# K chunks in pairs of neighbouring places, w4 in runs of seven rows

## The chip, the cores and the metric

The kernel runs on one core of one Trainium2 chip. The metric is the time of one execution in microseconds, as the device measures it; the time of a kernel is the median of its runs.

## The reference

Four blocks run one after the other over a batch of 8, with one query position: attention with a cached K and V, an MLP, and both once more with the same weights and the same caches. All inputs are bf16.

```python
def _A_ref(x, k_cache, v_cache, wq, wo):       # D 448, Hq 16, Hkv 8, Sk 4096, Dh 256
    q = (x @ wq)...                             # 16 heads, two for each of 8 K/V heads
    scores = jnp.einsum("bhqd,bhkd->bhqk", q, k) * (Dh ** -0.5)
    p = _softmax(scores, axis=-1)
    o = jnp.einsum("bhqk,bhkd->bhqd", p, v)
    return o... @ wo
def _B_ref(x, w1, w2, w3, w4):
    ...                                         # hs: shifts along S, zero for S = 1
    x1 = x + hs
    h2 = _gelu(_layernorm(x1, axis=-1) @ w3) @ w4      # w3 448 x 1792, w4 1792 x 448
    return x1 + h2
x = A_x
x = x + _A_ref(_layernorm(x, axis=-1), ...)
x = x + _B_ref(_layernorm(x, axis=-1), ...)
x = x + _A_ref(_layernorm(x, axis=-1), ...)
x = x + _B_ref(_layernorm(x, axis=-1), ...)
```

K and V of one batch row are 16.8 MB each, so the two passes over the caches could ask for 537 MB. Since S is 1, the shifted quarters of the MLP's first half are all zero, and w1 and w2 take no part.

## The kernel before

**Units and chunks.** The heads are taken in pairs of K/V heads: four pairs (gp 0 to 3) for each of 8 batch rows b, in two passes (ps 0 and 1). A unit (ps, b, gp) has four K chunks and four V chunks of 1 MB: 128 partitions of 8192 B. Chunk c of K holds rows 16c to 16c+15 of the 64 consecutive rows that each partition has of K; two neighbouring chunks c and c+1 are therefore one run of 16384 B per partition in HBM. In SBUF lie 17 places of a chunk's size side by side in one tile, `places_t`; two chunks can be loaded by one DMA if their places are neighbours.

**What is kept.** For the head pairs 2 and 3 (`keep`) the K chunks and most V chunks of pass 0 stay in their places, or in part in PSUM, and pass 1 of the same batch row uses them from there; these items need no load (`here`). Head pairs 0 and 1 are loaded in both passes.

**The order.** `items` is a list of 522 items, written out at build time by `block`, `first_kept` and `weights`: for each unit its K chunks and, some way behind, its V chunks, with those of other units between; an item with kv 2 is a block of wq or wo. For each batch row, after the units of pass 0, a stretch of V chunks alone follows (`narrow`), during which the dependent chain of that row (`chain`: softmax denominators, wo, layernorm, w3, gelu, w4, q of pass 1) is worked off in small steps between halves of V chunks. Most of those V chunks are loaded in two halves (`halved`).

**The planner.** All loads are issued by the sync engine (SP), in the order of `loads`, which is `items` without those that are kept. `emit_loads` (line 930) runs after each item and issues loads as long as places are free. `both_for` (line 900) decides on a pair: the two chunks must be within the next three loads, two neighbouring places must be free or come free within `AHEAD = 4` items, and at least `QUEUED = 7` loaded chunks must be waiting for their use; then the places are held, and nothing else is issued until both are free. If not, `place_for` (line 873) takes a single place, and tries to hold a neighbour of it for the mate, so that the score products can still read both chunks as one operand. An item gives its place back when its last product has been issued (lines 1463 to 1476); a pair of chunks whose scores are formed together (`late`) gives both back after the second.

**What an item does.** A loaded K chunk is turned in place by VectorE (L1009, three instructions). Scores are formed by TensorE (L1024): 32 matmuls with 256 columns for two chunks in neighbouring places, 64 with 128 columns for two others; `paired` says which units form them two by two. ScalarE takes the exponentials (L1033). A V chunk is multiplied in 16 matmuls (L1092), those of the last units in 32 (L1108), where V is the weight operand and every second column of it is taken.

**The MLP.** w3 lies in SBUF as three blocks of 128 rows with all 1792 columns, and a last block in which the 64 remaining rows stand twice, one half of the columns on the upper and one on the lower 64 partitions (`split_tile`). `wblk` gives the 128 columns 128c to 128c+127 of block fc as the weight operand; there are 14 x 4 = 56 such products in `mlp_hidden` (L471 and following; through `wide`, L180, for one batch row) and in the last MLP (L1550). w4 lies as `w4_sb[p, c, :]` = row 128c + p, loaded at line 1159:

```python
nc.sync.dma_start(w4_sb[:], B_w4.rearrange("(c p) d -> p c d", p=128))
```

The hidden values of column group c stand on the 128 partitions and meet `w4_sb[:, c]`, so the order of the columns in w3's products and that of the rows in w4 must agree.

Of the kernel before, what the change touches and what calls it, by code (L numbers as in the profile page):

```python
# [17 lines left out]
def kernel(  # L18
# [27 lines left out]
    nc = tc.nc  # L46
# [3 lines left out]
    Dh = A_k_cache.shape[3]  # L50
# [10 lines left out]
    NC = 17  # L61
# [160 lines left out]

    def rows_to_cols(row, nb):

# [236 lines left out]
    def mlp_hidden(b0, nb):  # L464

        yield from norm(xT[:, :, b0 : b0 + nb], nb, True)
        h_ps = room_ps("h", nb)
        for c in range(HC):
            for fc in range(4):
                w, xi = wblk(w3_sb, F, c, fc)  # L470
                if nb == 1:  # L471
                    wide(h_ps[:, c : c + 1], w, xbs(1)[:, xi, :], fc == 0, fc == 3)
                    continue
                nc.tensor.matmul(
                    h_ps[:, c * nb : c * nb + nb],
                    w,
                    xbs(nb)[:, xi, :],
                    start=(fc == 0),
                    stop=(fc == 3),
                )  # L480
            if c in (4, 9, HC - 1) if nb == 1 else c % 7 == 6:
                yield 0 if c == HC - 1 else None
        g_t = chn.tile([128, HC * MID], FP32, tag="g")
        hh = g_t[:, 0 : HC * nb]
        g0 = g_t[:, HC : 2 * HC] if nb == 1 else misc[:, 456 : 456 + HC * nb]
        if nb == 1:
            HT_t = chn.tile([128, HC, 1], BF16, tag="HT")
            HT = HT_t[:]
        else:
            HT = HTw[:, :, b0 : b0 + nb]  # L490

        nc.vector.tensor_scalar_mul(hh, h_ps, 0.5)
        nc.vector.scalar_tensor_tensor(g0, hh, 4 * 0.044715, hh, ALU.mult, ALU.mult)
        nc.vector.scalar_tensor_tensor(g0, g0, 1.0, hh, ALU.add, ALU.mult)
        nc.scalar.activation(g0, g0, ACT.Tanh, scale=2 * 0.7978845608028654)
        yield 0
        nc.vector.scalar_tensor_tensor(
            HT,
            g0.rearrange("p (c b) -> p c b", b=nb),
            1.0,  # L500
            hh.rearrange("p (c b) -> p c b", b=nb),
            ALU.add,
            ALU.mult,
        )
        yield 2
        return HT
# [337 lines left out]
    where = {}  # L844

    held = {}
    AHEAD = 4
    QUEUED = 7

    def paired(n, c):  # L850

        ps, _, gp = tasks[n]
        return gp in keep or tasks[n] in saved or tasks[n] in final_units[:2] + begin[1:]

    def late(it):

# [13 lines left out]
    free_at = [-1] * NC  # L870
    now = [0]

    def place_for(it):

        n, kv, c = it
        if it in held:
            p = held.pop(it)
            if p not in places:
                held[it] = p
                return None  # L880
            places.remove(p)
        else:
            open_ = [p for p in places if p not in held.values()]
            if not open_:
                return None
            p = open_[0]
            if kv == 0 and c % 2 == 0 and paired(n, c):
                two = [
                    (max(free_at[q], now[0]), k, p1, q)
                    for k, p1 in enumerate(open_)  # L890
                    for q in (p1 + 1, p1 - 1)
                    if 0 <= q < NC and q not in held.values() and free_at[q] <= now[0] + AHEAD
                ]
                if two:
                    _, _, p, q = min(two)
                    held[n, 0, c + 1] = q
            places.remove(p)
        return p

    def both_for(it):  # L900

        n, kv, c = it
        mate = (n, 0, c + 1)
        if it not in held:
            if kv or c % 2 or not paired(n, c) or mate not in loads[:3]:
                return None
            open_ = [p for p in range(NC) if p in places or free_at[p] >= 0]
            two = [
                (max(free_at[q] if q not in places else -1 for q in (p, p + 1)), p)
                for p in open_  # L910
                if p + 1 in open_ and not {p, p + 1} & set(held.values())
            ]
            two = [t for t in two if t[0] <= now[0] + AHEAD]
            if not two or sum(used_at[i] > now[0] for i in where if i in used_at) < QUEUED:
                return None
            p = min(two)[1]
            held[it], held[mate] = p, p + 1
        if held.get(mate) != held[it] + 1:
            return None
        return held[it], mate  # L920

    def taken(it, p):

        where[it] = p
        n, kv, c = it
        if stays(it):
            where[tasks[n][1:], it[1:]] = p
        free_at[p] = again[tasks[n][1:], kv, c] if tasks[n][0] == 0 and stays(it) else used_at[it]

    def emit_loads(most=None):  # L930
        n = 0
        while loads and places and n != most:
            it = loads[0]
            both = both_for(it)
            if both:
                p, mate = both
                if p not in places or p + 1 not in places:
                    break
                for i, q in ((it, p), (mate, p + 1)):
                    loads.remove(i)  # L940
                    places.remove(q)
                    del held[i]
                    taken(i, q)
                _, b, gp = tasks[it[0]]
                nc.sync.dma_start(
                    places_t[:, p * PB : (p + 2) * PB],
                    A_k_cache[b, 2 * gp : 2 * gp + 2]
                    .rearrange("g s d -> (g s) d")
                    .rearrange("(p u z) d -> u p (z d)", u=2, z=32)[it[2] // 2],
                )  # L950
                n += 1
                continue
            p = place_for(it)
            if p is None:
                break
            del loads[0]
            taken(it, p)
            t, kv, c = it
            _, b, gp = tasks[t]
            dst = slots[p]  # L960
            n += 1
            if kv == 2:
                load_weights(dst, gp, b)
                continue
            rows = (A_v_cache if kv else A_k_cache)[b, 2 * gp : 2 * gp + 2].rearrange(
                "g s d -> (g s) d"
            )
            if kv:
                src = rows.rearrange("(a p y) d -> a p (y d)", a=4, y=16)[c]
            else:  # L970
                src = rows.rearrange("(p x y) d -> x p (y d)", x=4, y=16)[c]
            if halfway(it):
                nc.sync.dma_start(dst[:, 0 : PR * Dh], src[:, 0 : PR * Dh])
                nc.sync.dma_start(rest_t[:], src[:, PR * Dh :])
            elif loads and it not in halved:
                nc.sync.dma_start(dst, src)
            else:
                for y in range(2):
                    nc.sync.dma_start(
                        dst[:, 8 * Dh * y : 8 * Dh * (y + 1)], src[:, 8 * Dh * y : 8 * Dh * (y + 1)]  # L980
                    )

    def load_tail(dst, src):

# [171 lines left out]
        A_wo[WI * 128 :].rearrange("(h p j) d -> p h (j d)", p=128, j=2),  # L1156
    )
    load_split(w3_sb, B_w3, F)
    nc.sync.dma_start(w4_sb[:], B_w4.rearrange("(c p) d -> p c d", p=128))
    run(norm(xT[:], Bn, False))  # L1160

    gens, pairs_done, p_of = [], {}, {}
# [109 lines left out]
    for idx, it in enumerate(items):  # L1272
# [190 lines left out]
        if kv == 2:  # L1463
            if gp == "q" or rows is not None:
                places.append(p)
        elif not (ps == 0 and stays(it)):
            if (ps, gp, kv, c) == (1, keep[1], 1, homes[0]):
                where[(b, part[0]), part[1:]] = p
                moves.extend(part_words(slot))
            elif (ps, gp, kv, c) == (1, keep[1], 1, homes[1]):  # L1470
                where[(b, inner[0]), inner[1:]] = p
                moves.extend(inner_words(slot))
            elif not late(it):
                places.append(p)
            elif c % 2:
                places.extend([where[n, 0, c - 1], p])
# [69 lines left out]
    for f0, f1 in ((0, 3), (3, 4)):  # L1546
        for c in range(HC):
            for fc in range(f0, f1):
                w, xi = wblk(w3_sb, F, c, fc)
                nc.tensor.matmul(  # L1550
                    h_ps[:, c * nb : c * nb + nb],
                    w,
                    xe[:, xi, :],
                    start=(c + fc == 0),
                    stop=(fc == 3),
                    skip_group_check=True,
                )
# [80 lines left out]
```

## Time and profile before

| | |
|---|---|
| median of three runs | 1040.58 us (1037.08 to 1041.28) |
| the profiled execution | 1038.57 us, its span 1036.0 us |
| read from HBM | 419.63 MB, 405 GB/s over the span |
| DMA packets | 73472 |
| busy: PE, DVE, ACT, POOL | 668.8, 597.9, 211.5, 16.3 us |
| mean granted clock of TensorE | 0.614 |

The span goes from the first to the last instruction of the core; the execution's time also holds what lies around it. In the groups of instructions, PE is a matmul and PEld the load of its weight operand, "busy" is the time of a group together and the mean is that of one instruction, overlaps counted. SPq is the queue of the sync engine: an issue of a DMA stands there at the time at which SP got to it, waits included. The views by stretch give, for each 10 us, the busy time of every engine, then the granted clock, the mean share of the 16 DMA engines that had a packet, and GB/s. The records of single packets (start, duration, size, queue) lie behind that share.

### The profile page before, as it was taken

How to read it: one execution, taken by the hardware profiler on the slowest of the kernel's cores; microseconds unless marked ns; L12 is line 12 of the kernel's file. 1: busy time of each engine (PE TensorE's matmuls, PEld its weight loads, DVE VectorE, ACT ScalarE, POOL GpSimd, SP SyncE). 2: the span in 40 equal slices, each digit the busy share in tenths (PEclk: the TensorE clock that was granted, in tenths of full speed). 3: DMA queues.
4: the chain of work that ended last, by engine and by line, in shares of the span. 5: the costliest groups of instructions: out<-in, count | busy, mean ns of one | idle time of the engine just before them, and what ended most of it. 6: DMA issues, size and time to landing. Idle time of an engine off the chain costs nothing. (4 is left out here: it accounts for less than half of the span.)

```text
span 1036.0 us, 29893 instructions
## 1 busy us (share of the span) xinstructions
PE 668.8 (65%) x13219; PEld 429.1 (41%) x13219; DVE 597.9 (58%) x1407; ACT 211.5 (20%) x685; POOL 16.3 (2%) x27
## 2 busy tenths in 40 slices
PE   3154545875677557766775677567756774677775
PEld 2022322553345334533453345335533552345555
DVE  7054577258725971597259725782597259725582
ACT  1011111141214120412041214121412141214110
POOL 0000000000000000000000000000000000000000
PEclk9975555565667566655665565566555665556555
DMA  9999999999999999999999999999999999999994
GB/s 361 396 425 422 423 422 419 393 421 419 419 401 421 422 417 382 419 422 419 401 415 425 417 402 411 421 417 388 418 420 418 401 419 423 417 402 408 413 419 198
DMA packets 73472, 421.56 MB, mean 407 GB/s; under 512 B 7544, under 2 KB 13440, under 8 KB 43904
## 3 DMA queue, kind: packets, MB, share of 16 engines
q1 hardware_dynamic: 73296, 419.66, 99.1%
q8 instruction: 103, 1.69, 0.7%
q14 instruction: 25, 0.20, 0.0%
q10 hardware_dynamic: 48, 0.01, 0.0%
HBM read 419.63 MB, written 0.01 MB: 405 GB/s over the span
## 5 line engine op out<-in xcount | busy, mean ns | idle before, releaser
L1009 DVE STREAM_TRANSPOSE places<-places 128x512 uint32<-128x512 uint32 (+1 forms) x576 | 455.5, 854 | 58.8 <-DMA places<-in_A_k_cache_dram 58.6
L1024 PE MATMUL sc<-places,qbd 128*8 128x256 bf16 (+1 forms) x5248 | 248.8, 342 | 175.4 <-DVE places L1009 168.5
L1092 PE MATMUL o<-places,ptw 128*8 128x256 bf16 x3808 | 243.7, 380 | 111.5 <-DMA places<-in_A_v_cache_dram 82.2
L1024 PEld LDWEIGHTS <-qbd 128*8 128x8 bf16 x5248 | 134.0, 105 | 247.0 <-DVE places L1009 130.6
L1092 PEld LDWEIGHTS <-ptw 128*8 128x8 bf16 x3968 | 103.9, 102 | 175.1 <-issue 99.0
L1033 ACT ACTIVATE p_n<-sc 128x256 bf16<-128x256 f32 x128 | 95.5, 746 | 341.2 <-PE sc L1024 335.7
L1267 ACT COPY ptw<-psv 128x32 bf16<-128x32 bf16 x248 | 53.1, 227 | 175.0 <-PE o L1092 173.0
L415 DVE CAST qbd<-misc 32x16 bf16<-32x16 f32 (+1 forms) x184 | 30.8, 167 | 63.2 <-PE misc L409 61.4
L592 PE MATMUL misc<-R_t,o_t 128*128 128x4 f32 (+1 forms) x212 | 45.5, 321 | 29.2 <-DVE qbd L415 12.8
L592 PEld LDWEIGHTS misc<-R_t,o_t 128*128 128x128 f32 x212 | 41.2, 271 | 45.2 <-issue 17.3
L1082 ACT CAST psv<-misc 128x128 bf16<-128x128 f32 x64 | 17.0, 265 | 198.8 <-PE misc L1075 198.8
L532 DVE RECIPROCAL rz<-misc 128x4 f32<-128x4 f32 (+1 forms) x55 | 9.7, 176 | 80.4 <-PE misc L529 43.6
L1060 ACT COPY places<-store 128x1024 bf16<-128x1024 bf16 x40 | 40.2, 1029 | 11.2 <-PE o L1092 10.7
L529 PE MATMUL misc<-zm,one 128*128 128x4 f32 (+1 forms) x110 | 28.0, 326 | 15.0 <-DVE zm L521 12.6
L529 PEld LDWEIGHTS misc<-zm,one 128*128 128x128 f32 x110 | 23.2, 263 | 30.8 <-DVE zm L521 15.9
L180 PEld LDWEIGHTS <-w_sb 128*128 128x128 bf16 x896 | 27.5, 104 | 15.7 <-issue 15.7
L1033 ACT ACTIVATION_READ_ACCUMULATOR p_n<-sc 128x1 f32 x128 | 33.8, 264 | 0.0
L546 ACT COPY o_t<-o 128x256 f32<-128x256 f32 x53 | 19.7, 373 | 49.5 <-PE o L1092 49.5
L295 POOL TENSOR_TENSOR t<-t,nhalf 128x2 f32<-128x2 f32 (+2 forms) x18 | 12.0, 669 | 955.5 <-DVE t L316 955.5
L1075 PEld LDWEIGHTS <-p_n 128*128 128x128 bf16 x256 | 11.9, 105 | 32.4 <-issue 20.9
L1055 DVE TENSOR_SCALAR store<-places 128x512 uint32<-128x512 uint32 x40 | 25.0, 679 | 0.0
L1075 PE MATMUL misc<-identb,p_n 128*128 128x32 bf16 x256 | 18.1, 191 | 10.3 <-ACT p_n L1033 6.8
(158 smaller groups left out, 358.7 us busy)
## 6 DMA issues: line engine op xcount, KB each, us to landing
places<-in_A_k_cache_dram SPq DMA_DIRECT2D x49, 2048.0 KB, 17.2
places<-in_A_v_cache_dram SPq DMA_DIRECT2D x194, 512.0 KB, 7.2
places<-in_A_k_cache_dram SPq DMA_DIRECT2D x94, 1024.0 KB, 12.0
places<-in_A_v_cache_dram SPq DMA_DIRECT2D x87, 1024.0 KB, 20.9
places<-in_A_wq_dram SPq DMA_DIRECT2D x7, 768.0 KB, 9.8
rest<-in_A_v_cache_dram SPq DMA_DIRECT2D x8, 640.0 KB, 18.5
places<-in_A_v_cache_dram SPq DMA_DIRECT2D x8, 384.0 KB, 14.8
wo_sb<-in_A_wo_dram SPq DMA_DIRECT2D x1, 2688.0 KB
```

Of the source, the lines that this page charges most:

```text
L180: nc.tensor.matmul(bass.AP(out.tensor, out.offset, [out.ap[0], (1, WIDE)]), w, x.to_broadcast([128, WIDE]), start=start, stop=stop, skip_g ...
L415: nc.vector.tensor_copy(qbd[32 * a : 32 * a + 32, :, g0 : g0 + ng, a, :], qs.rearrange("p e (f g u h) -> p (e f) u g h", f=2, u=2, h=2)[:, ...
L529: nc.tensor.matmul(z_ps, ones, zm[:], start=True, stop=True)
L592: nc.tensor.matmul(ot_ps[:, j], o_sb[:].rearrange("p (i j) -> p j i", j=2)[:, j], R, start=True, stop=True)
L1009: nc.vector.transpose(w, w)
L1024: nc.tensor.matmul(sc[32 * k : 32 * k + 8, 128 * (x % 2) : 128 * (x % 2 + nx)], qbd[:, ep, gp % 2].rearrange("p a h -> p (a h)"), v, start ...
L1033: nc.scalar.activation(p_sb[:, :, :, 2 * u : 2 * u + 2].rearrange("p t i x -> p x t i"), sc[:, 0:256].rearrange("p (x t i) -> p x t i", x= ...
L1055: nc.vector.tensor_single_scalar(kept_words.bitcast(U32), words.bitcast(U32), 0, op=ALU.bitwise_or)
L1060: nc.scalar.copy(words, kept_words.bitcast(BF16))
L1075: nc.tensor.matmul(pt_ps[:, t], p_sb[:, t].rearrange("p i x -> p (i x)"), cols, start=True, stop=True,)
L1092: nc.tensor.matmul(o_ps[32 * q : 32 * q + 8, :], ptz[:, at : at + 8], v[:, y * Dh : (y + 1) * Dh] if v2 is None or y < PR else v2[:, (y - ...
L1267: nc.scalar.copy(ptw[:, ring_of[it], :, 6:8], psv[slot_of[it[0]]][:, it[2]])
```

## The change

It has four parts.

- The planner. `place_for` and `both_for` go. `reserve` holds two neighbouring places for a pair if both are free or come free within `SOON = 8` items, and either both are free now or at least `QUEUED = 5` loaded chunks are waiting for use; the mate may stand up to three loads behind. While a pair is held and one of its places is not free, nothing is issued. A single load takes the free place with the fewest free neighbours (`pick`). Chunks 1 and 2 of a unit go together when chunk 1 was left single, the next load is chunk 2 and the next place is free.
- `paired` now holds for all units of `begin` and `final_units`.
- Kept K chunks in pass 1, whose scores are formed two by two after the first, give both places back at that time.
- w4 is loaded so that each partition has seven consecutive rows for each half of the 1792 rows, and `w3blk` takes every seventh column of w3: group c = 7u + j has columns 896u + j, 896u + j + 7, and so on.

```diff
+    def w3blk(c, fc):
+        u, j = divmod(c, HC // 2)
+        at = F // 2 * u if fc < 3 else 0
+        return w3_sb[:, fc * F + at + j : fc * F + at + F // 2 : HC // 2], (fc if fc < 3 else 4 - u)
...
-                w, xi = wblk(w3_sb, F, c, fc)
+                w, xi = w3blk(c, fc)
...
-    AHEAD = 4
-    QUEUED = 7
+    SOON = 8
+    QUEUED = 5
...
-        return gp in keep or tasks[n] in saved or tasks[n] in final_units[:2] + begin[1:]
+        return gp in keep or tasks[n] in saved or tasks[n] in final_units + begin
...
-    def place_for(it):
...
-    def both_for(it):
...
+    def open_places():
+        return [p for p in places if p not in held.values()]
+    def pick(open_):
+        return min(open_, key=lambda p: ((p - 1 in open_) + (p + 1 in open_), p))
+    def reserve(it, mate):
+        open_ = open_places()
+        taken_ = set(held.values())
+        def at(p):
+            return max(-1 if q in places else free_at[q] for q in (p, p + 1))
+        two = [
+            p
+            for p in range(NC - 1)
+            if not {p, p + 1} & taken_
+            and all(q in places or 0 <= free_at[q] <= now[0] + SOON for q in (p, p + 1))
+        ]
+        if not two:
+            return
+        p = min(two, key=lambda p: (at(p), sum(q in open_ for q in (p - 1, p + 2)) % 2, p))
+        queued = sum(used_at[i] > now[0] for i in where if i in used_at)
+        if at(p) <= now[0] or queued >= QUEUED:
+            held[it], held[mate] = p, p + 1
...
+    def load_k(it, p, n):
+        _, b, gp = tasks[it[0]]
+        rows = A_k_cache[b, 2 * gp : 2 * gp + 2].rearrange("g s d -> (g s) d")
+        nc.sync.dma_start(
+            places_t[:, p * PB : (p + n) * PB],
+            rows.rearrange("(p z) d -> p (z d)", z=64)[:, it[2] * PB : (it[2] + n) * PB],
+        )
...
     def emit_loads(most=None):
         n = 0
         while loads and places and n != most:
             it = loads[0]
-            both = both_for(it)
...
+            k, kv, c = it
+            mate = (k, 0, c + 1)
+            if kv == 0 and c % 2 == 0 and paired(k, c) and mate in loads[:4]:
+                if it not in held:
+                    reserve(it, mate)
+                if it in held:
+                    p = held[it]
+                    if p in places and p + 1 in places:
+                        del held[it], held[mate]
+                        taken(it, p)
+                        taken(mate, p + 1)
+                        load_k(it, p, 2)
+                        n += 1
+                        continue
+                    break
+            open_ = open_places()
+            if not open_:
+                break
+            p = pick(open_)
+            taken(it, p)
+            n += 1
+            if kv == 2:
+                load_weights(slots[p], tasks[k][2], tasks[k][1])
+            elif kv:
+                load_v(it, slots[p])
+            else:
+                both = c == 1 and (k, 0, 2) in loads[:2] and p + 1 in open_
+                if both:
+                    taken((k, 0, 2), p + 1)
+                load_k(it, p, 1 + both)
...
-    nc.sync.dma_start(w4_sb[:], B_w4.rearrange("(c p) d -> p c d", p=128))
+    nc.sync.dma_start(
+        w4_sb[:].rearrange("p (u j) d -> p u (j d)", u=2),
+        B_w4.rearrange("(u p j) d -> p u (j d)", u=2, p=128),
+    )
...
+            elif kv == 0 and kept_now:
+                if c % 2 == 0:
+                    places.extend([p, where[(b, gp), (0, c + 1)]])
             elif not late(it):
                 places.append(p)
...
-                w, xi = wblk(w3_sb, F, c, fc)
+                w, xi = w3blk(c, fc)
                 nc.tensor.matmul(
                     h_ps[:, c * nb : c * nb + nb],
```

V chunks are loaded as before, by the same DMAs (`load_v`).

More of the change, by code (lines that the diff above doesn't have):

```diff
@@ L871 @@
     now = [0]
-    def place_for(it):
[L875 to L898, printed above, removed]
@@ L900, in both_for @@
-    def both_for(it):
[L902 to L916, printed above, removed]
+    def open_places():
+        return [p for p in places if p not in held.values()]
@@ L917, in both_for @@
             held[it], held[mate] = p, p + 1
-        if held.get(mate) != held[it] + 1:
-            return None
-        return held[it], mate
     def taken(it, p):
@@ L928, in taken, with load_v @@
         free_at[p] = again[tasks[n][1:], kv, c] if tasks[n][0] == 0 and stays(it) else used_at[it]
+        if kv == 2 and tasks[n][1] is None:
+            free_at[p] = -1
+        loads.remove(it)
+        places.remove(p)
+    def load_k(it, p, n):
[5 more added lines that the diff above has]
+        )
+    def load_v(it, dst):
+        _, b, gp = tasks[it[0]]
+        rows = A_v_cache[b, 2 * gp : 2 * gp + 2].rearrange("g s d -> (g s) d")
+        src = rows.rearrange("(a p y) d -> a p (y d)", a=4, y=16)[it[2]]
+        if halfway(it):
+            nc.sync.dma_start(dst[:, 0 : PR * Dh], src[:, 0 : PR * Dh])
+            nc.sync.dma_start(rest_t[:], src[:, PR * Dh :])
+        elif loads and it not in halved:
+            nc.sync.dma_start(dst, src)
+        else:
+            for y in range(2):
+                nc.sync.dma_start(
+                    dst[:, 8 * Dh * y : 8 * Dh * (y + 1)], src[:, 8 * Dh * y : 8 * Dh * (y + 1)]
+                )
     def emit_loads(most=None):
@@ L933, in emit_loads @@
             it = loads[0]
-            both = both_for(it)
-            if both:
-                p, mate = both
-                if p not in places or p + 1 not in places:
-                    break
[L939 to L952, printed above, removed]
@@ L953, in emit_loads @@
-            p = place_for(it)
-            if p is None:
+            k, kv, c = it
[12 more added lines that the diff above has]
+                        continue
+                    break
@@ L955, in emit_loads @@
+            open_ = open_places()
+            if not open_:
                 break
-            del loads[0]
+            p = pick(open_)
             taken(it, p)
-            t, kv, c = it
-            _, b, gp = tasks[t]
-            dst = slots[p]
             n += 1
             if kv == 2:
[L963 to L967, printed above, removed]
@@ L968, in emit_loads @@
-            if kv:
-                src = rows.rearrange("(a p y) d -> a p (y d)", a=4, y=16)[c]
-            else:
[L971 to L981, printed above, removed]
+                load_weights(slots[p], tasks[k][2], tasks[k][1])
+            elif kv:
+                load_v(it, slots[p])
+            else:
+                both = c == 1 and (k, 0, 2) in loads[:2] and p + 1 in open_
+                if both:
+                    taken((k, 0, 2), p + 1)
+                load_k(it, p, 1 + both)
@@ L1158 @@
     load_split(w3_sb, B_w3, F)
-    nc.sync.dma_start(w4_sb[:], B_w4.rearrange("(c p) d -> p c d", p=128))
+    nc.sync.dma_start(
+        w4_sb[:].rearrange("p (u j) d -> p u (j d)", u=2),
+        B_w4.rearrange("(u p j) d -> p u (j d)", u=2, p=128),
+    )
     run(norm(xT[:], Bn, False))
```

## The prediction

> **What bounds the kernel now.** I read the slices of the page first, then the DMA queues and issues, the chain that ended last, the busy time by stretches of 10 us, the waits of the sync engine's queue, and the weight loads by shape.
>
> ```profile
> DMA  9999999999999999999999999999999999999994
> GB/s 361 396 425 422 423 422 419 393 421 419 419 401 421 422 417 382 419 422 419 401 415 425 417 402 411 421 417 388 418 420 418 401 419 423 417 402 408 413 419 198
> q1 hardware_dynamic: 73296, 419.66, 99.1%
> ```
>
> The 16 DMA engines have packets from the first slice to the last but one. The packet records add up: the durations of all packets, over 16 engines, make 1034.7 us of a span of 1036.0 us. No engine's busy time comes near that (PE 668.8, DVE 597.9). So the time is the sum of the packets, plus what stands after the last transfer:
>
> ```profile
> 1007.79 17.29 DMA places<-in_A_v_cache_dram
> ...
> 1028.49 1.64 PE store L1550 x56
> ...
> 1033.06 0.27 DVE places L1603
> ```
>
> The last data lands at 1025.1 us, and some 11 us of dependent work follow; in it stand the 56 products with w3 (L1550), 29 ns each. There, and only there, work of TensorE lies on the path for sure. Everything else matters through the DMA queue: how cheap its packets are, and whether it ever runs empty.
>
> ```profile
> places<-in_A_k_cache_dram SPq DMA_DIRECT2D x49, 2048.0 KB, 17.2
> ...
> places<-in_A_k_cache_dram SPq DMA_DIRECT2D x94, 1024.0 KB, 12.0
> ...
> w_sb<-in_B_w_dram SPq DMA_DIRECT2D x1, 1568.0 KB, 15.1
> ```
>
> A K chunk is 1 MB, 8192 B per partition and packet; a pair is one DMA of 128 packets of 16384 B. Of 192 K chunks that are loaded, 98 go in pairs now. The w4 load moves rows of 896 B, 1792 packets.
>
> **Part 1, more pairs.** I walked the lists of both planners over the 522 items (they depend on no time). The old rules give 49 pairs and 94 single chunks, as the rows above show; the new ones give 86 DMAs of two chunks (7 of them chunks 1 and 2 of a unit) and 20 singles: 37 DMAs become one where they were two. From the packet records, a mean packet of 8192 B on this queue takes 315.0 ns (23,168 of them) and one of 16384 B 616.9 ns (6,272). Each engine carries 8 packets of a chunk: two chunks cost 16 x 315.0 = 5040 ns, a pair 8 x 616.9 = 4935 ns. Saved: 105 ns a pair, and 9 ns for one semaphore packet per engine less: 114 ns x 37 = **4.2 us**. The medians (312 and 613) give 88 + 9 = 97 ns, 3.6 us. That the gap belongs to the packets and not to quiet stretches is seen within one stretch: from 60 to 160 us, where the queue is deep, the means are 314.2 and 616.6. I take the means over the run, since the singles that go lie in stretches of all kinds.
>
> **Part 2, w4 in runs of seven rows.** 1792 packets of 896 B at 46.1 ns over 16 engines make 5.2 us. They become 256 packets of 6272 B; the records show 5120 B at 200.5 ns and 8192 B at 315, so by a straight line 243 ns: 3.9 us. Saved: **1.3 us**, at 30 to 43 us of the span, where the DMA share stands at 1.04 to 1.07 and nothing else sets the pace.
>
> **Part 3, w3 read in every seventh column.** The number of weight loads and products stays (56 per use, ten uses). Whether a load that steps 14 bytes takes longer the trace does not show; it shows steps of 4 and 8 bytes:
>
> ```profile
> L592 PEld LDWEIGHTS misc<-R_t,o_t 128*128 128x128 f32 x212 | 41.2, 271 | 45.2 <-issue 17.3 <-ACT o_t L546 15.2 <-DVE R_t L575 6.8
> L180 PEld LDWEIGHTS <-w_sb 128*128 128x128 bf16 x896 | 27.5, 104 | 15.7 <-issue 15.7
> L529 PEld LDWEIGHTS misc<-zm,one 128*128 128x128 f32 x110 | 23.2, 263 | 30.8 <-DVE zm L521 15.9 <-issue 8.5 <-DVE qT L379 1.7
> L1108 PEld LDWEIGHTS <-places 128*128 128x128 bf16 x256 | 7.7, 105 | 5.0 <-DMA places<-in_A_v_cache_dram 4.8 <-issue 0.2
> ```
>
> L1108 reads every second bf16 column and takes 105 ns against 104 for packed w_sb; L592 reads every second f32 and takes 271 against 263 (L529). So 0 by the nearest rows, and that is what I take. It can't gain, since no load goes away. The upper end is a load that moves no faster than an f32 one: 41.2/212 = 194 ns of busy time each against 1.8/56 = 32 for w3 at the end; 162 ns x 56 = 9.1 us in the tail. In the eight rounds of the chain the 56 products stand between halves of V chunks, hidden as long as PE keeps up: from 293 to 303 us it is busy 8.4 of 10 us.
>
> The Trainium skill speaks against a price of nothing: by "SBUF — State Buffer", section "Door 1: The DMA port swizzle", memory lines are 16 bytes long and full bandwidth needs at least two hits in a line. A step of 14 bytes gives about one hit a line; steps of 4 and 8 bytes give four and two, and there the rows agree with it. (The page also counts 8 bf16 as a free step, so it can be read both ways.)
>
> **Part 4, the order and the holding back.** A pair now waits for two neighbouring places when five chunks are ahead and both places come free within 8 items, and while it waits, everything behind it on SP waits too, V chunks among them. What hides this is the queue's stock. For each DMA of the new order I took the end of the item that lets it go, as the trace has it, and counted what had been issued before it less what had landed. The thinnest place is at 646 us:
>
> ```profile
> 634.79 0.33 SPq L945 DMA_DIRECT2D places<-in_A_k_cache_dram  x1
> 635.17 1.86 SPq L976 DMA_DIRECT2D places<-in_A_k_cache_dram  x2
> 642.96 0.33 SPq L976 DMA_DIRECT2D places<-in_A_v_cache_dram  x1
> 647.53 0.33 SPq L945 DMA_DIRECT2D places<-in_A_k_cache_dram  x1
> ```
>
> Before the V issue at 642.96 the queue held 3.69 MB. The two chunks of L976 at 635.17 become a pair that waits until 645.8, and the V stands behind it: 3.69 - 2.10 - 2.84 us x 0.42 MB/us = 0.4 MB, 1.0 us of work left when it goes out. The next thinnest such places have 0.95, 1.13, 1.34, 1.51, 1.67 and 1.80 MB (2.3 to 4.3 us). None is empty, so no stall. A thin stock by itself costs little: the stretch at 550 us, where 1.8 MB stood, ran at 416 GB/s against 420. For 12 such places of some 5 us each, 1% is 0.6 us; I take 0.5.
>
> Against it, kept K chunks give their two places back after the first of them and not one by one. Where the narrow V stretch ends, the old order ran thin, and the new one issues earlier there:
>
> ```profile
> 620.00:630.00 10.00, 7.68 (x158) 5.18 (x161) 1.72 (x11) 1.96 (x7) 0.00 (x0) 0.67 1.01 401
> 630.00:640.00 10.00, 7.72 (x114) 5.46 (x104) 4.86 (x16) 4.59 (x12) 0.00 (x0) 0.50 1.02 410
> 640.00:650.00 10.00, 7.75 (x149) 4.57 (x149) 7.17 (x15) 4.94 (x12) 0.00 (x0) 0.50 1.01 426
> ```
>
> (The last number is GB/s.) Filling all such stretches (210, 310, 410 to 430, 520, 620 to 640, 720 to 740, 830 and 940 us) up to 420 would be worth 1.8 us; between 0 and that I take 1.2. At the start 9 MB of K and V stand ahead of the weights and not 5, but the V chunk at which the weights are first needed (the thirteenth item) comes after the same bytes, so nothing waits.
>
> The score products of nine more couples of chunks go in 32 matmuls and not 64, twelve chunks of other units likewise; PE is not on the path there, so 0. No queue but SP's has DMAs moved on it.
>
> **Sum:** -4.2 - 1.3 + 0 + 0.5 - 1.2 = -6.2 us. The profiled execution took 1038.57 us, 2.6 us around its span of 1036.0; it becomes 1032.4. The median of the runs shown is 2.0 us higher, 1040.58; from it, **1034.4 us**.
>
> **Rivals.**
> - *A column alone in its line doubles the weight load.* 32 ns more x 56 in the tail: +1.8 us; in the chain 32 x 56 = 1.8 us a round against 1.6 us that PE has free and a stock of 1 MB (2.4 us), so nothing more. Time 1036.2. For it: 14 bytes is beyond any step the rows show. Against: 4 and 8 bytes cost nothing at all. The Trainium skill's page on SBUF, read strictly, would make this of it.
> - *The saving in packets is not had.* If a longer packet only does well where the queue is deep, the 37 new pairs, many of which go out into a thin queue, save their semaphores alone (0.3 us); with w4's 1.3 and the thin stretches at 0.5, nothing for the earlier release: -1.1, 1039.5. Against it stands the comparison within one stretch.
> - *The held pair starves the queue; slower.* Both chunks of a pair land together, so the first is turned up to 2.5 us later than now, the places come free later, and the wait for the next pair grows by that. If the releases come L us later than in this trace, the stalls are the sum of L minus the stock at each thin place. L = 2.5 costs 1.5 + 0.2 = 1.7 us; L = 3.8 costs 6.2 and eats the gain; L = 5 costs 15 us, so 1049. For it: DVE is busy 9 to 10 tenths where K chunks come thick (360 to 380, 550 to 590 us), so it can't catch up there. Against: a chunk that is used later finds both landed.
> - *Weight loads at the f32 pace.* 9.1 us in the tail; in each round 9.1 us of PE against 1.6 us free and 2.4 us of stock, so 5 us of empty queue, 40 us in eight rounds: some 1083. It decides from 110 ns more a load, where the tail alone takes the gain.
>
> **How the numbers follow.** My forecast has 0.58; the doubled load 0.09, the packets that save nothing 0.15, the starved queue 0.12, the f32 pace 0.06. A measurement of this kernel tells about 0.5% from no change, 5.2 us, so faster means under 1035.4. The forecast's own range is 1031 to 1038 (the medians for the means, 0 to 1.8 us for the earlier release, 0 to 2 for the thin places); three quarters of its chance lie under 1035.4: 0.44 faster. The rest of it, 0.14, with the second and third cases, makes 0.38 without a change that shows; the last two make 0.18 slower. The range reaches from 1030 (all of the gains with none of the costs, and a median of before as low as its lowest run) to 1046, which takes in a queue that starves by up to 12 us and leaves out the deeper cases.
>
> **What would show it.** Right: 86 K issues of 2048 KB and 20 of 1024 KB; 256 packets of 6272 B where w4's 1792 short ones were; the queue's packets adding up to about 5.5 us less; L1550's line still 1.6 us; DMA tenths of 9 throughout. Wrong: a stretch with a DMA share under 1.00 near 646 or 471 us (starving), weight loads from w_sb over 104 ns, or 16384 B packets well over 617 ns.

## The result, and the profile after

The changed kernel takes 1041.18 us (median of 22 runs, 1038.74 to 1045.28) against 1038.80 us before (22 runs on the same chips): ratio 1.0022, 95% interval 1.0013 to 1.0031. By the ratio it is 2.3 us slower; 1034.4 us was forecast, from the first median of 1040.58.

The page of the changed kernel, slices, main queue and issues:

```profile
GB/s 371 402 425 423 422 423 418 378 426 425 416 403 425 424 411 374 423 423 416 401 414 426 416 386 413 424 417 386 425 424 415 386 420 427 414 378 418 418 421 170
...
q1 hardware_dynamic: 66432, 419.66, 98.7%
...
places<-in_A_k_cache_dram SPq DMA_DIRECT2D x86, 2048.0 KB, 14.2
...
places<-in_A_k_cache_dram SPq DMA_DIRECT2D x20, 1024.0 KB, 11.8
```

The pairs are there, 86 and 20, and 6,864 packets are gone from the queue. The same bytes move. But of the eight dips, one in every fourth slice, where the V stretch with the chain lies, six are deeper: 378, 374, 386, 386, 386 and 378 where before had 393, 382, 402, 388, 401 and 402. The mean of the eight is 386.5 GB/s against 396.3. One slice of one execution says little, so the means of the runs below stand beside them: 397.3 in e3, which has the new planner without w3's steps, and 386.5 in e2, which has the steps without the planner.

The busy time by stretches of 10 us in three of these V stretches, and from 640 to 650 us, after; the last three numbers are TensorE's granted clock, the mean share of the DMA engines with a packet, and GB/s:

```profile
390.00:400.00 10.00, 8.82 (x151) 5.89 (x154) 1.94 (x11) 0.66 (x3) 0.70 (x1) 0.50 0.91 320
610.00:620.00 10.00, 7.25 (x166) 4.70 (x163) 2.52 (x14) 1.15 (x5) 0.55 (x1) 0.67 1.00 362
640.00:650.00 10.00, 7.17 (x227) 5.28 (x227) 7.26 (x15) 4.79 (x12) 0.00 (x0) 0.84 1.01 414
920.00:930.00 10.00, 8.71 (x190) 5.64 (x179) 2.62 (x15) 1.25 (x6) 0.55 (x1) 0.50 0.99 334
```

The same stretches before:

```profile
390.00:400.00 10.00, 7.19 (x145) 4.48 (x142) 2.05 (x12) 0.66 (x3) 0.70 (x1) 0.53 1.01 389
610.00:620.00 10.00, 7.61 (x172) 4.86 (x169) 2.51 (x14) 1.15 (x5) 0.55 (x1) 0.67 1.01 394
640.00:650.00 10.00, 7.75 (x149) 4.57 (x149) 7.17 (x15) 4.94 (x12) 0.00 (x0) 0.50 1.01 426
920.00:930.00 10.00, 8.34 (x183) 5.35 (x183) 2.83 (x16) 1.14 (x5) 0.55 (x1) 0.50 1.02 406
```

At 646 us, where a held pair was expected to drain the queue, the share stays at 1.01. From 610 to 620 and from 920 to 930 us the DMA engines have packets all the time (1.00 and 0.99) and yet move less than before: the packets last longer. From 920 to 930 us the mean packet of 4096 B, half a V chunk's, takes 192 ns, before 164.

Only from 390 to 400 us is the share of these four under 0.99, and that dip is there without w3's steps too. It begins at 389 us, and the products with w3 of this round at 395 us. The queue's stock (bytes issued so far, less those of the packets that have ended) is down to 0.62 MB at 388.5 us. In e1, whose w3 is packed, it is 0.63 MB there, and that slice of the page is at 374 GB/s too. In the profiles of the changed kernel, e1, e3 and e4 a V load goes out near 385 us only 8.6 to 10.1 us after the one before it, and the stock falls to 0.54 to 1.00 MB. In e7 and e8, with the same planner, it is 6.9 and 6.7 us and 1.46 MB or more, as before the change (6.9 us, 1.48 MB). So it belongs to the new planner, but why it comes in some executions only stays open.

What changed inside is the weight load. The loads of w3 and w4 in the chain, and of w3 in the last MLP, after; then w3 in the last MLP before:

```profile
L180 PEld LDWEIGHTS <-w_sb 128*128 128x128 bf16 x896 | 40.0, 128 | 19.0 <-issue 18.1
...
L1553 PEld LDWEIGHTS <-w_sb 128*128 128x128 bf16 x56 | 3.3, 155 | 0.6 <-issue 0.6
```

```profile
L1550 PEld LDWEIGHTS <-w_sb 128*128 128x128 bf16 x56 | 1.8, 107 | 0.6 <-issue 0.6
```

A load that steps 14 bytes has 3.3/56 = 59 ns of busy time and not 32; the granted clock is 0.50 in both. In the chain half of the 896 loads are of w3: (40.0 - 27.5)/448 = 28 ns more each. The page "SBUF — State Buffer" of the Trainium skill (section "Door 1: The DMA port swizzle"), in its strict reading of two hits per 16-byte line, agrees with this, though it names no price; its other reading, that a step of up to 8 bf16 is free, does not hold here: 7 costs 27 ns. That the lines are the reason is not shown: no step but 2, 4 and 14 bytes was run for bf16.

The chain that ended last, at its end, after:

```profile
1029.73 3.11 PE store L1553 x56
...
1034.24 1.51 PE store L1597 x43
...
1035.78 0.27 DVE places L1606
```

The 56 products with w3 took 1.64 us before and take 3.11 now. All of that is on the path: from the last data to the last instruction of the chain it is 9.7 us, before 8.2.

### The profile page after: what moved, and what is told of

It reads as the page before. It is cut to its first block, busy times and chain, and to the rows that moved or that the text cites. A ratio compares the mean times of both kernels' runs of the same rounds, so it can differ in the third digit from the quotient of the medians.

```text
span 1038.9 us, 28857 instructions
## 1 busy us (share of the span) xinstructions
PE 674.1 (65%) x12739; PEld 434.6 (42%) x12739; DVE 597.6 (58%) x1407; ACT 211.1 (20%) x685; POOL 16.4 (2%) x27
## 3 DMA queue, kind: packets, MB, share of 16 engines
q8 instruction: 100, 1.64, 0.6%
## 4 chain that ended last, share of the span: by engine, by line
DMA 40%; DVE 28%; PE 26%; ACT 2%; issue 2%; SPq 1%; POOL 0%; DVEq 0%; ACTq 0%
DMA places<-in_A_v_cache_dram 26%; DVE places L1006 22%; DMA places<-in_A_k_cache_dram 12%; PE sc L1021 8%; PE o L1089 8%; PE misc L180 4%; PE misc L598 2%; ACT p_n L1030 1%; DVE store L1052 1%; DVE qbd L421 1%; PE misc L535 1%; DMA w_sb<-in_B_w_dram 1%; DMA places<-in_A_wq_dram 1%; SPq L199 1%; PE misc L459 1%
## 5 line engine op out<-in xcount | busy, mean ns | idle before, releaser
L1021 PE MATMUL sc<-places,qbd 128*8 128x256 bf16 (+1 forms) x4768 | 239.1, 355 | 159.8 <-DVE places L1006 157.8
L1021 PEld LDWEIGHTS <-qbd 128*8 128x8 bf16 x4768 | 125.2, 105 | 227.9 <-DVE places L1006 121.1
L1089 PEld LDWEIGHTS <-ptw 128*8 128x8 bf16 x3968 | 101.1, 102 | 179.1 <-issue 102.6
L180 PEld LDWEIGHTS <-w_sb 128*128 128x128 bf16 x896 | 40.0, 128 | 19.0 <-issue 18.1
L180 PE MATMUL misc<-xb,w_sb 128*128 128x32 bf16 x448 | 28.4, 216 | 1.3 <-DVE xb L330 1.3
```

Of the source, the lines that this page charges most:

```text
L180: nc.tensor.matmul(bass.AP(out.tensor, out.offset, [out.ap[0], (1, WIDE)]), w, x.to_broadcast([128, WIDE]), start=start, stop=stop, skip_g ...
L1021: nc.tensor.matmul(sc[32 * k : 32 * k + 8, 128 * (x % 2) : 128 * (x % 2 + nx)], qbd[:, ep, gp % 2].rearrange("p a h -> p (a h)"), v, start ...
L1089: nc.tensor.matmul(o_ps[32 * q : 32 * q + 8, :], ptz[:, at : at + 8], v[:, y * Dh : (y + 1) * Dh] if v2 is None or y < PR else v2[:, (y - ...
```

## The experiments

Ratios are to the kernel before, run beside them; in brackets the 95% interval.

**Which half does it.** Three kernels split the change, and a fourth places the loss. e1 has the new planner with w3 and w4 as before, e2 the reverse, e3 all but the steps of seven in w3, e4 steps of seven in the last MLP only.

```diff
 e1, e3, e4 (e4: in mlp_hidden alone), from the changed kernel
-                w, xi = w3blk(c, fc)
+                w, xi = wblk(w3_sb, F, c, fc)
 e1 besides
-    nc.sync.dma_start(w4_sb[:].rearrange("p (u j) d -> p u (j d)", u=2), ...)
+    nc.sync.dma_start(w4_sb[:], B_w4.rearrange("(c p) d -> p c d", p=128))
 e2, from the kernel before: w3blk and w4's new load
```

> The changed kernel with w3 and w4 as before: w3's 128 consecutive columns as the weight operand, w4 in rows of 896 B. Theory A (the new planner earns its packets, the strided weight loads give it back): the K packets are 3.6 us cheaper as in the changed kernel's records and the semaphores 0.35 us, so about 4 us faster than before, ratio 0.996. Theory B (holding pairs back thins the queue and costs what the packets save): no faster, ratio 1.000 to 1.002.

> The kernel before with the new w4 load and w3's columns by sevens, its planner untouched. Theory A: +1.5 us in the tail (56 loads at 59 in place of 32 ns), about 4 us in the eight V stretches of the chain, -1.3 us for w4's packets: 4 us slower, ratio 1.004. Theory B: only the tail less w4's packets, +0.2 us, ratio 1.000.

> The changed kernel, planner and w4 load included, with 128 consecutive columns of w3 as the weight operand in all products: the hidden columns then meet other rows of w4, so another function is computed by the same instructions. Theory A: -4 us for the K pairs and -1.3 us for w4: ratio 0.995. Theory B: -1.3 us to +1 us, ratio 0.999 to 1.001.

> The changed kernel with consecutive columns of w3 in the chains of the eight batch rows (and the MLP of rows 0 to 3 at the end), and columns by sevens in the last MLP alone; the hidden columns of the former meet other rows of w4, so another function is computed. Theory A with most of the loss in the chains: 1.5 us above the kernel with w3 packed everywhere, so ratio about 0.9965 to before. If the loss were in the tail alone, the ratio would be that of the changed kernel, 1.002. Theory B: 1.000 to 1.002.

| | us, median | ratio |
|---|---|---|
| e1, planner only | 1037.60 | 0.9993 (0.9982 to 1.0004) |
| e2, w3 and w4 only | 1043.01 | 1.0039 (1.0026 to 1.0052) |
| e3, all but the strided w3 | 1036.78 | 0.9982 (0.9970 to 0.9994) |
| e4, strided in the last MLP only | 1038.34 | 0.9994 (0.9984 to 1.0005) |

e2 is where theory A put it; theory B falls there, since w3 and w4 alone cost 4.1 us. From e3 to the changed kernel the strided loads cost 0.0040, 4.2 us (2.6 to 5.8). Of that 1.2 us (-0.4 to 2.9) are the tail's (e3 to e4), where the trace has 1.5. The other 2.9 us (1.5 to 4.4) are those of the rounds before it, with the MLP of rows 0 to 3 among them, which e4 has packed too. But e1 misses theory A and lies nearer to B: the planner gives 0.7 us and not 4. e3 and e4 miss theory A by the same 3 us; e3 lies between the two theories.

**Is it TensorE's time, or the strided read?** e7 keeps w3 packed and issues each of its products in the chain twice.

```diff
-  wide(h_ps[:, c : c + 1], w, xbs(1)[:, xi, :], fc == 0, fc == 3)
+  wide(h_ps[:, c : c + 1], w, xbs(1)[:, xi, :], fc == 0, False)
+  wide(h_ps[:, c : c + 1], w, xbs(1)[:, xi, :], False, fc == 3)
```

> The changed kernel with 128 consecutive columns of w3 in all products, and in the chains of the eight batch rows each of the 56 products with w3 issued twice, so that the hidden values count double: 56 x 37 ns = 2.1 us more of TensorE per round, with packed loads. If the strided loads cost their time by keeping TensorE from the V chunks (theory C), this costs at least as much in the rounds as they do, 2.9 us or more over the packed kernel: ratio to before 1.001 or more. If it is the strided read itself that disturbs the transfers into SBUF (theory D), nothing: ratio 0.998.

1.0026 (1.0015 to 1.0037), 0.0044 or 4.6 us above e3 (2.9 to 6.3). The products with w3 in the chain, before, in the changed kernel and in e7:

```profile
L180 PE MATMUL misc<-xb,w_sb 128*128 128x32 bf16 x448 | 16.7, 190 | 0.0
```

```profile
L180 PE MATMUL misc<-xb,w_sb 128*128 128x32 bf16 x448 | 28.4, 216 | 1.3 <-DVE xb L330 1.3
```

```profile
L180 PE MATMUL misc<-xb,w_sb 128*128 128x32 bf16 x896 | 28.8, 189 | 0.8 <-DVE xb L330 0.8
```

The doubled products were expected to take 2.1 us more a round; they take 1.5 (28.8 against 16.9 us in e3, over eight rounds), just what the strided loads take. So e7 holds TensorE as long as the changed kernel does, with packed loads, and costs at least as much: 0.57 us a round, where the strided loads cost 0.36 (rows 0 to 3 counted in). Nothing is left for theory D to explain. Between a quarter and two fifths of TensorE's time comes through to the end; the two figures don't differ by more than their intervals. How the chain stands between the V chunks is seen in TensorE's timeline (start, duration, instructions, and in brackets the idle time before and what ended it), changed kernel, then before in another round:

```profile
395.23 1.29 PE L180 MATMUL misc<-xb,w_sb 128*128 128x32 bf16 x20 [0.85 <-DVE xb L330]
396.72 0.59 PE L1089 MATMUL o<-places,ptw 128*8 128x256 bf16 x8 [0.20 <-DMA places<-in_A_v_cache_dram]
397.25 1.25 PE L180 MATMUL misc<-xb,w_sb 128*128 128x32 bf16 x20
398.43 0.60 PE L1089 MATMUL o<-places,ptw 128*8 128x256 bf16 x8
398.96 1.04 PE L180 MATMUL misc<-xb,w_sb 128*128 128x32 bf16 x16
```

```profile
293.80 0.77 PE L180 MATMUL misc<-xb,w_sb 128*128 128x32 bf16 x20
294.55 0.60 PE L1092 MATMUL o<-places,ptw 128*8 128x256 bf16 x8
295.08 0.73 PE L180 MATMUL misc<-xb,w_sb 128*128 128x32 bf16 x20
```

Twenty products took 0.77 us before and take 1.29. Half a V chunk is now followed by the next after 1.71 us (396.72 to 398.43), while DMA brings one in about 1.25 us. TensorE falls behind, the places come free late, and the next V loads go out late. The stock shows it. From the V issue before the first product with w3 to the one after the last it falls in each of the eight rounds, by 0.40 MB in the mean (from 292.3 to 296.5 us, 1.70 to 1.31 MB). It falls by 0.39 MB in e2 and by 0.38 in e7, whose loads are packed; before the change and in e3 it stays (+0.07 and -0.03 MB).

The loss shows in the V packets. Those of 4096 B, 25,216 in each kernel, add up, over 16 engines, to 260.9 us before and 261.7 in e3, to 264.3 in the changed kernel and in e2, and to 266.9 in e7. The differences to e3 are 2.6 us and, for e7, 5.2 us; the times gave 2.9 and 4.6 us. What makes a packet longer in a thin queue, the records don't tell.

**What is a pair worth?** e5 issues each of the 86 pairs of e1 as two DMAs, e9 each of the 49 of the kernel before; order and places stay.

```diff
+        for k in range(n):
             nc.sync.dma_start(
-            places_t[:, p * PB : (p + n) * PB], ...
+                places_t[:, (p + k) * PB : (p + k + 1) * PB], ...
```

> The new planner alone (w3 and w4 as before) with the same places, order and holds, but each of its 86 pairs issued as two DMAs of 1 MB. Theory A1 (a pair's packets are worth the 105 ns and the semaphore packet 9 ns that the records show, and holding places back has eaten some 3 us of it): 86 x 114 ns = 9.8 us slower than the planner alone, ratio to before 1.0087. Theory A2 (the longer packet by itself saves little, a K packet's time depends on the queue it stands in): 0 to 2 us slower than the planner alone, ratio 0.999 to 1.001.

> The kernel before with each of its 49 pairs issued as two DMAs of 1 MB, its order untouched. If a pair is worth the 114 ns of the packet records: 5.6 us slower than before, ratio 1.0054. If it is worth the 37 ns that splitting 86 pairs cost: 1.8 us slower, ratio 1.0017.

e5: 1.0024 (1.0013 to 1.0035), 3.2 us above e1, 37 ns a pair (19 to 56); theory A2 had at most 2 us. e9: 1.0030 (1.0020 to 1.0041), 3.1 us, 64 ns a pair (42 to 87). Neither is 114. In e5's profiled execution the packets' durations do add up to 9.1 us more than in e1 (1034.1 and 1025.0 us over 16 engines), as A1 had it. In the times 3.2 us of it appear; the two profiled executions differ by 6.6 us, but e5's is the longest of its nine. A stream of loads with no computation measures it alone:

```diff
+    for go in range(2):                       # e11: WIDTH 1, e12: WIDTH 2
+        for b in range(8): ...                # K and V, 537 MB, 16 places in turn
+                        nc.sync.dma_start(
+                            places_t[:, at * PB : (at + WIDTH) * PB],
+                            src[:, c * PB : (c + WIDTH) * PB])
+                        at = (at + WIDTH) % NC
```

> All computation left out: 512 loads of 1 MB, K and V caches twice over, 537 MB, packets of 8192 B, into 16 places in turn; the output is zero. At the pace of the deep stretches, 2.4 to 2.5 us per MB: 1270 to 1300 us. The kernel to compare with is the next one.

> The same bytes as 256 loads of 2 MB, packets of 16384 B; all computation left out, the output is zero. If a pair is worth 114 ns by itself, 29 us less than with loads of 1 MB; if 37 ns, 9.5 us less. If the difference in packet durations is overlap of packets and not time, nothing.

1281.11 us (1280.80 to 1281.28) against 1260.63 us (1260.09 to 1260.78): 20.5 us for 256 pairs, **80 ns a pair**. The main queue of each, packets, MB and share of 16 engines:

```profile
q1 hardware_dynamic: 73744, 536.91, 100.8%
```

```profile
q1 hardware_dynamic: 36880, 536.89, 100.2%
```

With short packets the queue is busy 100.8% of the span: a packet's record runs on while the next on its engine has begun. The sums of the records differ by 28.4 us (111 ns a pair), the times by 20.5. Durations of packets don't simply add up to time.

**Does a thin queue eat the rest?** e6 lets the planner hold places only half as long; e13 to e15 are the streams with few loads in flight.

```diff
 e6
-    SOON = 8
+    SOON = 4
 e13, e14 (1 MB loads), e15 (2 MB loads)
-    NC = 16
+    NC = 2            # e14: 3; e15: 4
```

> The new planner alone with SOON = 4 in place of 8: by the walk over its lists 66 DMAs of two chunks and 60 singles, and 18 in place of 32 K issues into a queue that holds less than 2.3 MB. Theory A1: 20 pairs fewer cost 2.3 us, and most of the 3 us that holding costs come back: about as fast as the planner alone or 1 us faster, ratio 0.998 to 0.9995. Theory A2: neither matters, ratio 0.999 to 1.000.

> The stream of 1 MB loads (all computation left out, output zero) into two places in turn, so a load goes out when the last but one has landed, with 1 MB still queued. If a stock of 1 MB is enough, as I took it: 1281 us as with eight loads in flight, at most 1% more. If a queue that thin loses time: several per cent more, as in the stretches of the kernel that run at 390 to 400 GB/s, some 1340 us.

> The same with three places: 2 MB still queued when a load goes out. If stock is what matters, near 1281 us.

> The stream of 2 MB loads (all computation left out, output zero) with two loads in flight, 2 MB still queued when one goes out. If a pair keeps its 80 ns in a thin queue: near 1261 us. If a thin queue takes the gain of the long packets away: 1281 us or more.

e6: 0.9995 (0.9984 to 1.0005), the same as e1, 20 pairs fewer and little more than half as many thin places; it tells the theories not apart.

The streams tell more. With three places of 1 MB, or two of 2 MB, nothing is lost: e14 1280.83 us, e15 1260.40 us, as in e11 and e12; a pair keeps its 80 ns there. With two places of 1 MB the same loads take 1610 to 1779 us (four runs; the profiled one is the longest). From 400 to 600 us, e13:

```profile
400.00:600.00 200.00, 0.00 (x0) 0.00 (x0) 1.00 0.80 302
```

and e14:

```profile
400.00:600.00 200.00, 0.00 (x0) 0.00 (x0) 1.00 1.01 421
```

The stock by the packets is less than the places suggest: at an issue 1.2 to 1.8 MB are still to come in e14, 1.4 to 1.9 in e15, but only 0.06 to 0.88 MB in e13. The landing marks show how. A load is spread over the 16 engines, and each marks its end. In e13 fifteen marks of a load come 4.0 to 4.5 us after the end of its issue (medians), the last only at 6.6 us: one of the sixteen runs behind by 2.1 us, most of the 2.5 us that a load lasts in e11. SP starts the next issue 0.02 us after that last mark; the issue takes 0.33 us, and the idle engines start again 0.65 us later. Before about every second issue no more than three engines still had a packet. The packets are longer as well, 348 ns in the mean and not 314.

So a place that is free only at the last mark leaves less in the queue than the bytes counted, and with under 0.9 MB in it the stream of 1 MB loads loses time. Between 0.9 and 1.2 MB nothing was measured. In the V stretches before the change the stock at the issue of half a V chunk was 0.87 MB at the least and 1.56 in the median; in the changed kernel 0.62 and 1.57. An issue there waits for a matmul and not for a landing, so how much of e13's loss holds for it is not shown.

**A version with the order by sevens made once.** e8 sorts w3's columns at the start, while GpSimd has nothing else to do, and takes packed columns from then on; its w3 blocks land in buffers that are free then, and wo is loaded last. e10 is the same on the planner of before.

```diff
+    def load_sevens(fc, land):
+        nc.sync.dma_start(land, B_w3[fc * 128 : fc * 128 + 128, :])
+        nc.gpsimd.tensor_copy(
+            w3_sb[:, fc * F : (fc + 1) * F].rearrange("p (u j q) -> p u j q", u=2, j=HC // 2),
+            land.rearrange("p (u q j) -> p u j q", u=2, j=HC // 2))
+    load_sevens(2, wo_sb[:].rearrange("p h d -> p (h d)")[:, 0:F])
+    load_split(wq_sb, A_wq[:, HF:], HF)
+    load_sevens(0, rest_t[:, 0:F])
+    load_sevens(1, slots[tails][:, HF // 2 + F // 2 : HF // 2 + F // 2 + F])
...
-                w, xi = w3blk(c, fc)
+                w, xi = wblk(w3_sb, F, c, fc)
```

> The changed kernel with w3's columns put into the order by sevens once, at the start, by three copies on GpSimd and the copies of the last block on ScalarE; all products then take 128 consecutive columns and w4 stays in runs of seven rows. The weights are loaded in another order, wo last. Theory A: as fast as with w3 packed, ratio 0.998; the reference's function. If the copies or the order of the weights hold the queue up at the start, up to 5 us slower than that.

> The kernel before, old planner and all, with w4 in runs of seven rows and w3's columns sorted by sevens once at the start. w4's packets save 1.3 us and the products take packed columns: ratio 0.9987. Against the same with the new planner (0.9972) it tells what the planner gives: 1.4 us if a pair is worth 37 ns, 4.2 us if 114 (ratio 0.9987 would then have to be nearer 1.001).

e8: 1036.84 us, 0.9972 (0.9962 to 0.9982), by its ratio the fastest of all, 2.9 us under the kernel before and 5.2 under the changed one. e10: 1038.15 us, 0.9987 (0.9976 to 0.9999). Between them the planner is worth 1.6 us (0 to 3.1); e1 had 0.7. One of the three copies and the loads of the last MLP, e8:

```profile
L1157 POOL COPY w_sb<-wo_sb 128x1792 bf16<-128x1792 bf16 x1 | 2.9, 2937 | 32.9 <-DMA wo_sb<-in_B_w_dram 32.9
...
L1567 PEld LDWEIGHTS <-w_sb 128*128 128x128 bf16 x56 | 1.8, 107 | 0.6 <-issue 0.6
```

2.9 us of GpSimd each, and the load is back at 32 ns. Two of the copies, 5.8 us, do stand in the chain that ended last, at 39 to 45 us of the span, behind w3's load; the kernel is none the less not slower than e3, which has no copies.

## Why the prediction was wrong

Its sum was -6.2 us, and +2.3 was measured.

- **What bounds the kernel** was right: the DMA queue and the tail. Both of the losses came through these two.
- **Part 1, the count** was right to the DMA (86 and 20). **The size failed**: 114 ns a pair, taken from the mean durations of packets, is 80 ns of time in a full queue (e11, e12), 37 ns with the new planner (19 to 56, e5) and 64 ns in the kernel before (42 to 87, e9). The step that broke is "Each engine carries 8 packets of a chunk: two chunks cost 16 x 315.0"; the records overlap, as the page's share of over 100% for the stream shows. At 80 ns 37 pairs are 3.0 us, at 37 ns 1.4. Put otherwise, all 86 pairs together save 3.2 us, and the 49 of before already saved 3.1.
- **Part 2** was right: 256 packets of 6272 B at 243 ns mean, as worked out; e10 gives -1.3 us (-2.5 to -0.1), e3 against e1 -1.1.
- **Part 3 failed, and it decides the sign.** "So 0 by the nearest rows": steps of 4 and 8 bytes said nothing about 14. It costs 27 ns a load, 4.2 us in all. One of the rows was misread besides: L529's weights are one element repeated (a step of 0), not packed f32, so 271 against 263 ns said nothing of a step. The first rival had the load within 5 ns (32 ns, +1.8 in the tail; 1.5 in the trace) and had 0.09. But it too stopped at the tail: "1.8 us a round against 1.6 us that PE has free and a stock of 1 MB (2.4 us), so nothing more". Here stood 2.9 us. The stock was counted as cover to its last byte. In the changed kernel it never ran out in these steps: it fell by 0.4 MB, to 1.0 to 1.5 MB, and the V packets lasted longer all the same.
- **Part 4.** The held pairs starved nothing at the places named: 414 GB/s and a share of 1.01 at 640 to 650 us, 415 and 1.00 at 470 to 480. The planner as a whole was put at -4.9 us (-4.2, +0.5, -1.2) and gave -0.7 (e1: -1.9 to +0.4) to -1.6 (e8 less e10). With pairs at 37 ns, -1.4, that can be accounted for, and the 0.7 us of net gain from earlier releases did not show. What brings a pair's worth from 80 down to 37 ns stays open: e15 kept the 80 ns with 1.4 MB and more on their way, e6 did not separate it, and the intervals are as wide as the effect.
- **The rivals.** The second, that the packets' saving isn't had, was right in part. The fourth did not come. Of the third something did: where it named DVE as full, from 360 to 380 us, the pause between two V issues grows from 6.9 to 9.3 us and the stock falls to 0.62 MB, though not in every profile. That this comes of the held pairs is not shown.
- **The signs.** The 86 and 20 issues, the 256 packets and the DMA tenths came as said. The queue's packets add up to 2.0 us less and not 5.5: K's and their semaphores 3.7 and w4's 1.3, against 3.4 more for the V halves. L1550's line, L1553 now, takes 3.1 us and not 1.6, and the loads from w_sb went from 104 to 128 ns, which it had named as a sign of being wrong.
- **The chances.** Slower by 0.22% is within the 0.5% called no change, which had 0.38; the time lies in the range, the forecast of a gain was wrong.

With the measured terms the sum is: planner -0.7, w4 -1.1, tail +1.2, rounds +2.9: +2.3 us. These are steps from one run to the next, so they must add up; what tests them is e2, which has the last three alone: +3.0 by the terms, 4.1 (2.7 to 5.4) measured.

## What to carry to other kernels

A gain in DMA layout that asks another operand to be read with a step must be charged for that step at every place where it is read; if the order is fixed, sort once while an engine is idle. Cost a longer packet by the time of a stream of such packets, not by the difference of their durations. And do not count the stock of a DMA queue as cover to its last byte: here, where it stood at 1 to 2 MB, each microsecond of an engine that "has time" was paid for in part, a quarter to two fifths.

## What was not expected of the hardware

- A weight load of 128 bf16 columns at a step of 14 bytes takes 59 ns of TensorE's busy time, packed 32 ns, both at a granted clock of 0.50; at a step of 4 bytes (L1108) it was 30 ns.
- A stream of 1 MB loads runs at 421 GB/s with 1.2 to 1.8 MB on their way at each issue and at 302 GB/s (profiled execution) with 0.06 to 0.88 MB.
- In the latter one of the 16 DMA engines ran 2.1 us behind the others, and a load counts as landed only when the last has marked it.
- Packets of 16384 B stream at 428 GB/s and of 8192 B at 422, with nothing else running.
